# V rows by VectorE's 32x32 block transposes instead of TensorE transposes, in an attention block on one Trainium2 core

## The chip, the cores and the metric

The kernel runs on one core of one Trainium2 chip, as one program. The metric is the device time of one execution in microseconds, the median of several runs. All engines of the core work at once, each on its own queue in program order: TensorE (PE; its weight loads are shown apart as PEld), VectorE (DVE), ScalarE (ACT), GpSimd (POOL) and SyncE (SP), which here only issues DMAs. They wait for each other through semaphores.

## The reference

One transformer block with adaptive layer norm over 2048 tokens of width 512, 32 heads of 16, and a hidden layer of 1792, all in fp32:

```python
mod = (silu(c) @ w_mod)                       # six rows of 512: sa, ca, ga, sb, cb, gb
h = layernorm(x) * (1 + ca) + sa
qkv = (h @ wqkv)                              # 2048 x (3 * 32 heads * 16)
p = softmax(q @ k.T * 16 ** -0.5)             # per head, 2048 x 2048
x = x + ga * ((p @ v) @ wo)
h = layernorm(x) * (1 + cb) + sb
x = x + gb * (gelu(h @ w1 + b1) @ w2 + b2)
```

## The kernel before

Tokens are cut into NB = 4 blocks of TB = 512, heads into NG = 8 groups of four. A *unit* is one block of queries against one group of heads; there are NU = 32, in the order of query blocks, and in each 16 *steps*, one per chunk of 128 keys. Values are handled for two head groups at a time, so there are four value column sets k = 0 to 3 (128 columns, eight heads each); unit u uses set `u % 8 // 2`.

**Precision.** Projections and the later matrix products split each fp32 operand into a high and a low part and add three products (`terms3`): 12 matmuls for a 128x512 projection. In the attention phase each of them is cut into two halves of 64 rows, 24 matmuls of 64 rows.

**The script.** The first phase (about the first 100 us) is written out by hand in `SCRIPT`: tokens are names of operations (`ops`) with an engine letter. It normalizes and transposes x, projects what the first units need, and stores Q, K and V pieces to DRAM, from where they are loaded in the layout that the attention needs. Of the V projections it makes set 0: `G200`, `G201` and `G203` with `U`, `C` and `O` (transpose on TensorE, ScalarE's copy, store), and `G202` with `Y202` (`high_later`), which leaves the row block to be turned in the next phase.

**The attention phase.** `half_step(hs)` writes one step's instructions for every engine, 512 times. It holds four score matmuls `e` (L647) with ScalarE's exponentials `p` (L654), four matmuls `mx` (L390) of a later unit, whose row maxima VectorE reduces (`mxp`, L395), up to RUN = 6 background matmuls `bg` (L276) and, at its end, `pv_step`: the four heads' products with V (L681). Score, maximum and background matmuls use 64 rows each and run in pairs in the two halves of the array; the pv matmuls use all 128 rows and 32 columns each, the four heads side by side in the array's columns. Every one of them is two passes. Banks are taken in turn (`ring`, `take`): e has three, mx three, pv and bg one each.

The *background work* (`jobs`, from `work`) comes in groups of 24 half matmuls, four steps each. `block0` plans it: the rest of K and V of set 1, then Q, K and V of sets 2 and 3, then the rest of Q; weights are loaded and split two plan entries ahead. After that come the output projection and the hidden layer of earlier query blocks.

Work that follows a matmul group is put off by a clock that ticks once per exponential (four times a step): `later(n, f)` runs f n ticks on, `soon` does the same and counts it as owed, and `sides` holds work that is emitted at the end of a step, ahead of its pv matmuls.

**V, before.** `proj_v` has the projection of value set k for token block b in the order (128 columns) x (512 tokens); ScalarE copies it to `vr`; five ticks later `turn_v` waits in `sides`. It takes an mx bank, transposes four 128x128 pieces on TensorE (L335), ScalarE copies them in two instructions (L340) to `vst`, whose rows hold, for a head group and a 128-token chunk, four times 16 values and a one, and 15 zeros (VG = 83 floats). Four ticks later SP stores them to `v_d` (L345). `load_v` brings a unit's V back in two halves of 8 chunks (L601) into `vg`, two buffers in turn; each half needs the stores of its two token blocks. In `pv_step` the stationary operand of head j is the 32 columns from `j * VW`: 16 values, the one, whose product is the softmax denominator, and 15 columns that are not used.

Loads are emitted by `step_start` from the list `due`, each with the earliest step and the stores that it needs. SP issues its DMAs in program order and stands where one has to wait.

Of the kernel before, what the change touches and what calls it, by code (L numbers as in the profile page):

```python
# [8 lines left out]
F32 = mybir.dt.float32  # L9
# [22 lines left out]
VW = DH + 1  # L32
VG = 4 * VW + DH - 1
EPS = 1e-5
# [36 lines left out]
def block_kernel(ctx: ExitStack, tc: tile.TileContext, x, wqkv, wo, w1, b1, w2, b2, c, w_mod, out):  # L71
# [82 lines left out]
    wslots = [wpool.tile([P, 2, KC, P], FR, name=f"wqkv{i}") for i in range(4)]  # L154
    vst = wpool.tile([P, 2, 4, VG], F32, name="vst")
    scm, spool = pool("stage", side="right")
# [68 lines left out]
    gp.tensor_copy(sel_b, sel[:, :2, None].to_broadcast([P, 2, P]))  # L225
    gp.memset(vst[:, :, :, 4 * VW :], 0.0)
    for j in range(4):
        gp.memset(vst[:, :, :, j * VW + DH], 1.0)

# [45 lines left out]
    def mm(ps, term, i, n, r=slice(None)):  # L275
        return te.matmul(ps, term[0][r], term[1][r], start=i == 0, stop=i == n - 1)  # L276

# [22 lines left out]

    def proj_terms(w, k, b):
        hi, lo = hT[b]
        t = wt_of[w, k]
        n = range(KC)
        return terms3([t[:, 0, i] for i in n], [t[:, 1, i] for i in n], [hi[:, i] for i in n], [lo[:, i] for i in n])

# [9 lines left out]

    vrows, sides = [], []

    def proj_v(k, b):
# [10 lines left out]
    def turn_v(bk, apart=False):  # L330

        k, b, r, _ = vrows.pop(0)
        ps = take(bk)
        for t in range(4):
            te.transpose(ps[:, t * P : (t + 1) * P], r[:, t * P : (t + 1) * P], ident)  # L335

        def evac():
            p5 = ps.rearrange("p (t g j d) -> p g t j d", t=4, g=2, d=DH)
            for g in range(2):
                ac.activation(vst[:, g, :, : 4 * VW].rearrange("p t (j e) -> p t j e", e=VW)[:, :, :, :DH], p5[:, g], AF.Copy)  # L340
            return store

        def store():
            stored.add((2, k, b))
            (ac if apart else sy).dma_start(v_d[2 * k : 2 * k + 2, :, 4 * b : 4 * b + 4, :].rearrange("g p k e -> p g k e"), vst)  # L345

        if apart:
            return evac
        evac()
        soon(4, store)  # L350


# [49 lines left out]

    rows = {}

    def max_rows(u):
        m = mn[u % 2]
        ve.tensor_reduce(m[:, :16], mxp.pop(u), axis=AX.X, op=ALU.min)
        mt = small.tile([P, 32], F32, tag="mt", name="mt")
        ve.transpose(mt, m)
        m2 = small.tile([P, 2, 32], FR, tag="m2", name="m2")  # L410
        gp.tensor_copy(m2[:, 0], mt)
        gp.tensor_tensor(m2[:, 1], mt, m2[:, 0].bitcast(F32), op=ALU.subtract)

        def store():
            for i in range(2):
                sy.dma_start(m_d[u][i].rearrange("x b j -> b x j"), m2[:, i].bitcast(F32))

        def load():
            mrows.add(u)
            for a in range(2):  # L420
                r0 = a * 64 + KR
                sy.dma_start(qst[u][r0 : r0 + 2].bitcast(F32).rearrange("s p t -> s (p t)"),
                             m_d[u][:, a * 8 : a * 8 + 8].rearrange("s x b j -> s (x b j)"))
# [62 lines left out]
    def group(w, k, b):  # L486
        terms = proj_terms(w, k, b)
        keep["G", w, k, b] = ps = take("pr")
        for i, t in enumerate(terms):
            mm(ps, t, i, len(terms))  # L490

    def high(w, k, b, e):
        ps = keep["G", w, k, b]
        if w == 2:
            r = stage("vr")
            copy(e, r, ps)
            vrows.append((k, b, r, 0))
        else:
            keep["A", w, k, b] = parts = pieces("parts")
            copy(e, parts[:, 0], ps)  # L500
# [15 lines left out]
    def turn_values(w, k, b):  # L516
        keep["U"] = turn_v("pr", True)

# [39 lines left out]
    def high_later(w, k, b, e):  # L558
        r = spool.tile([P, D], F32, tag="vr", name="vr", bufs=STAGE["vr"])
        copy(e, r, keep["G", w, k, b])  # L560
        vrows.append((k, b, r, 0))
        sides.append(lambda: turn_v("mx"))

# [19 lines left out]
    assert not queue and len(vrows) == 1 and set(k[0] if isinstance(k, tuple) else k for k in keep) <= {"G", "c"}, keep  # L583
    load_w(2, 1)
# [6 lines left out]
    dvcm, dvpool = pool("div", side="right")  # L591
    vgcm, vgpool = pool("vg", bufs=2)
    ppcm, ppool = pool("p", bufs=10)
    vg, pt = {}, {}

    def load_v(u, h):
        assert all((2, u % NG // 2, b) in stored for b in (2 * h, 2 * h + 1))
        if h == 0:
            vg[u] = vgpool.tile([P, NKC, VG], F32, tag="vg", name="vg")
        sl = slice(8 * h, 8 * h + 8)  # L600
        sy.dma_start(vg[u][:, sl], v_d[u % NG][:, sl])  # L601

# [71 lines left out]
    def pv_step():  # L674
        s = cur["pv"]
        cur["pv"] += 1
        u, kc = divmod(s, NKC)
        if kc == 0:
            cur["ps"] = take("pv")
        for j in range(4):  # L680
            te.matmul(cur["ps"][32 * j : 32 * (j + 1)], vg[u][:, kc, j * VW : j * VW + 32], pt.pop(4 * s + j),  # L681
                      start=kc == 0, stop=kc == NKC - 1)
        if kc == NKC - 1:
            vg.pop(u)
            attn_out(u, cur["ps"])
# [77 lines left out]
    def until(cond):  # L763
        while not cond():
            yield None
# [203 lines left out]
    def block0():  # L969
# [13 lines left out]
        for n, (w, k, bs) in enumerate(plan):  # L983
# [6 lines left out]
            wt_of.pop((w, k))  # L990
        yield from until(lambda: not preps and not owed[0] and not vrows and not busy[0])
        open_ffn()
# [53 lines left out]
    def half_step(hs):  # L1046
# [102 lines left out]
    def step_start(s):  # L1149
# [10 lines left out]
        if kc == 0 and u + 1 < NU:  # L1160
            for h in range(2):
                need = [(2, (u + 1) % NG // 2, b) for b in (2 * h, 2 * h + 1)]
                due.append((16 * u + 2 + h, need, lambda h=h: load_v(u + 1, h)))
# [141 lines left out]
```

## Time and profile before

| | |
|---|---|
| median of 3 runs | 1686.44 us (1686.33 to 1686.57) |
| profiled execution's own time | 1688.23 us |
| its span on the core | 1686.4 us, 32218 instructions |
| mean granted TensorE clock | 0.996 |
| busy: PE, DVE, ACT, POOL | 1666.6, 1402.0, 1242.7, 691.2 us |
| mean busy share of the DMA engines (queue q1) | 50.9% |
| attention phase, first to last pv matmul | 104.9 to 1562.1 us |

The profile lists groups of instructions by line, engine, operation and tile: count, busy time in us, mean ns of one, then the idle time of the engine just before them and what ended it. Idle time of an engine that is not the bound costs nothing. A timeline row has start, duration, engine, line, operation, tiles, shape and count of merged instructions. "128*32" ahead of a shape is the array's rows times columns. A row of a source view has the least, median and greatest duration in ns behind the count.

### The profile page before, as it was taken

How to read it: one execution, taken by the hardware profiler on the slowest of the kernel's cores; microseconds unless marked ns; L12 is line 12 of the kernel's file. 1: busy time of each engine (PE TensorE's matmuls, PEld its weight loads, DVE VectorE, ACT ScalarE, POOL GpSimd, SP SyncE). 2: the span in 40 equal slices, each digit the busy share in tenths (PEclk: the TensorE clock that was granted, in tenths of full speed). 3: DMA queues.
4: the chain of work that ended last, by engine and by line, in shares of the span. 5: the costliest groups of instructions: out<-in, count | busy, mean ns of one | idle time of the engine just before them, and what ended most of it. 6: DMA issues, size and time to landing. Idle time of an engine off the chain costs nothing.

```text
span 1686.4 us, 32218 instructions
## 1 busy us (share of the span) xinstructions
PE 1666.6 (99%) x12103; PEld 915.8 (54%) x12103; DVE 1402.0 (83%) x2686; ACT 1242.7 (74%) x2386; POOL 691.2 (41%) x697
## 2 busy tenths in 40 slices
PE   7999999999999999999999999999999999999999
PEld 6655555555554455555545555555555555553777
DVE  7998888889889989888999888888999888890332
ACT  4367888878777788778877888778877788779131
POOL 7333534425121456415633456306633466226110
PEclk8999999999999999999999999999999999999999
DMA  8766766756457443425453464344363453243544
GB/s 291 220 195 186 236 194 200 227 182 206 146 159 215 121 106 102 106 67 150 123 162 88 114 165 121 84 133 134 105 181 86 116 144 101 75 119 97 209 153 157
DMA packets 137127, 251.88 MB, mean 149 GB/s; under 512 B 25854, under 2 KB 45324, under 8 KB 136972
## 3 DMA queue, kind: packets, MB, share of 16 engines
q1 hardware_dynamic: 135984, 248.53, 50.9%
q8 instruction: 96, 1.57, 0.4%
q10 hardware_dynamic: 988, 1.29, 0.3%
q14 instruction: 59, 0.48, 0.1%
HBM read 188.49 MB, written 61.28 MB: 148 GB/s over the span
## 4 chain that ended last, share of the span: by engine, by line
PE 95%; DMA 2%; DVE 1%; ACT 1%; issue 0%; POOL 0%; SPq 0%; DVEq 0%; POOLq 0%; ACTq 0%
PE bg L276 40%; PE pv L681 30%; PE e L647 16%; PE mx L390 5%; PE pr L276 2%; ACT p L654 1%; DVE mxp L395 1%; DMA wraw<-in_A_wqkv_dram 1%; PE o L276 1%; PE mx L335 0%; DMA wo<-wos 0%; DMA kh<-qk 0%; PE mx L879 0%; DMA xin<-in_A_x_dram 0%; POOL wqkv L208 0%
## 5 line engine op out<-in xcount | busy, mean ns | idle before, releaser
L395 DVE TENSOR_REDUCE mxp<-mx 128x1 f32<-128x512 f32 x2034 | 1286.4, 683 | 145.7 <-PE mx L390 131.4
L654 ACT ACTIVATE p<-e 128x512 f32<-128x512 f32 x2048 | 1072.8, 608 | 272.2 <-PE mx L390 251.4
L390 PE MATMUL mx<-kh,qst 48*128 48x512 f32 x2034 | 836.6, 423 | 0.7 <-DVE mxp L395 0.5
L647 PE MATMUL e<-qst,kh 50*128 50x512 f32 x2048 | 779.2, 424 | 3.2 <-ACT p L654 3.2
L647 PEld LDWEIGHTS e<-qst,kh 50*128 50x128 f32 x2048 | 341.8, 185 | 431.5 <-ACT p L654 310.2
L681 PE MATMUL pv<-p,vg 128*32 128x512 f32 x4096 | 547.2, 605 | 0.3 <-ACT osb L668 0.3
L390 PEld LDWEIGHTS mx<-kh,qst 48*128 48x128 f32 x2034 | 368.2, 185 | 14.2 <-DVE mxp L395 8.3
L276 PE MATMUL bg<-w,g 64*128 64x512 f32 (+1 forms) x1056 | 264.3, 389 | 0.8 <-issue 0.8
L276 PEld LDWEIGHTS bg<-w,g 64*128 64x128 f32 (+1 forms) x1056 | 196.0, 186 | 30.0 <-issue 1.2
L276 PE MATMUL bg<-pchi,w 64*128 64x512 f32 (+1 forms) x656 | 177.6, 391 | 0.0
L681 PEld LDWEIGHTS pv<-p,vg 128*32 128x32 f32 x4096 | 81.1, 108 | 173.0 <-issue 160.3
L276 PE MATMUL bg<-hThi,wqkv 64*128 64x512 f32 x560 | 153.1, 392 | 0.0
L276 PEld LDWEIGHTS bg<-pchi,w 64*128 64x128 f32 (+1 forms) x656 | 120.9, 185 | 23.9 <-DVE tick L1091 4.2
L276 PEld LDWEIGHTS bg<-hThi,wqkv 64*128 64x128 f32 x560 | 103.7, 185 | 12.7
L923 POOL TENSOR_SCALAR s<-s 128x512 f32<-128x512 f32 x40 | 59.9, 1497 | 90.3 <-ACT s L921 89.6
L942 POOL TENSOR_TENSOR x<-y,x 128x512 f32<-128x512 f32 x28 | 36.0, 1286 | 144.6 <-ACT y L941 128.7
L276 PE MATMUL bg<-pclo,w 64*128 64x512 f32 (+1 forms) x328 | 88.9, 389 | 0.0
L276 PE MATMUL bg<-hTlo,wqkv 64*128 64x512 f32 x280 | 76.5, 392 | 0.0
L276 PEld LDWEIGHTS bg<-pclo,w 64*128 64x128 f32 (+1 forms) x328 | 60.0, 184 | 13.5 <-DVE tick L1091 4.2
L916 POOL TENSOR_TENSOR s<-h 128x512 f32<-128x512 f32 x40 | 41.7, 1042 | 61.7 <-ACT h L915 61.7
L276 PE MATMUL bg<-wo,pchi 64*128 64x512 f32 x192 | 59.5, 389 | 0.4 <-DMA wo<-wos 0.4
L276 PEld LDWEIGHTS bg<-hTlo,wqkv 64*128 64x128 f32 x280 | 51.6, 184 | 7.5
(163 smaller groups left out, 1322.9 us busy)
## 6 DMA issues: line engine op xcount, KB each, us to landing
kh<-qk SPq DMA_DIRECT2D x256, 192.0 KB
w<-w1s SPq DMA_DIRECT2D x56, 512.0 KB
w<-w2s SPq DMA_DIRECT2D x54, 512.0 KB
vg<-v SPq DMA_DIRECT2D x64, 332.0 KB
qk<-parts SPq DMA_DIRECT2D x32, 512.0 KB
qst<-qk SPq DMA_DIRECT2D x64, 192.0 KB
qk<-parts SPq DMA_DIRECT2D x32, 256.0 KB
ou<-osb SPq DMA_DIRECT2D x32, 256.0 KB
```

The source lines that it names most:

```text
L276: return te.matmul(ps, term[0][r], term[1][r], start=i == 0, stop=i == n - 1)
L390: te.matmul(ps, qst[u][r0 : r0 + KR, p, qc * P : (qc + 1) * P], kh(u, kr // 2)[r0 : r0 + KR, p, (kr % 2) * TB : (kr % 2 + 1) * TB], start= ...
L395: ins = ve.tensor_reduce(mxp[u][:, hc, kr : kr + 1], ps, axis=AX.X, op=ALU.max, negate=True)
L647: ins = te.matmul(ps, kh(u, kc // 8)[r0 : r0 + KX, p, (kc % 8) * P : (kc % 8 + 1) * P], qst[u][r0 : r0 + KX, p], start=True, stop=True)
L654: op = ac.activation(t, ps, AF.Exp, scale=SCALE)
L681: te.matmul(cur["ps"][32 * j : 32 * (j + 1)], vg[u][:, kc, j * VW : j * VW + 32], pt.pop(4 * s + j), start=kc == 0, stop=kc == NKC - 1)
L916: gp.tensor_tensor(s, h, h, op=ALU.mult)
L923: gp.tensor_scalar(s, s, 1.0, None, op0=ALU.add)
L942: later(4, lambda: gp.tensor_tensor(x2[t], y, x2[t], op=ALU.add))
```

## The change

For thirteen of the sixteen V groups (the twelve of the attention phase and the one that the script leaves over) the transposes move from TensorE to VectorE, which turns 32x32 blocks inside SBUF. So that four blocks side by side end in rows that belong to one token chunk, the projection reads its tokens in another order: 16 runs of 32 tokens per matmul (`proj_terms(..., blocks=True)`, `mm`). `turn_block` turns one quarter of a group (128x128) with one VectorE instruction; `turn_blocks` is called at the end of each step, ahead of the pv matmuls, and spreads a group's four quarters over up to three steps, later when a unit's row maxima have just been emitted (`rowed`). The store follows two ticks after the last quarter.

The rows' layout changes too: four chunks are interleaved, so the 32 stationary columns of a head lie four floats apart in `vst`, `v_d` and `vg`, and a chunk's two heads take 2 * 17 floats with no padding. `vst` has two buffers after the script. `v_d` is one tensor per value set; sets 1 to 3 are stored with the block index leading and loaded in two DMAs by head pairs, each of which needs all four token blocks; set 0 is loaded in two halves of two token blocks. The two `vg` tiles are allocated once, with 60 zero floats at their ends. The three script groups that stay on TensorE write the new layout with ScalarE.

```diff
-v_d = dram.tile([NG, P, NKC, VG], F32, name="v")
+v_d = [dram.tile([4, P, NB, 4 * VB], F32, name=f"v{k}") for k in range(KC)]     # VB = 2 * VW
...
+    def store_v(k, b, apart=False):
+        stored.add((2, k, b))
+        t = vst[b % len(vst)]
+        rows = v_d[k][:, :, b]
+        if k:
+            sy.dma_start(rows.rearrange("q p e -> p q e"), t)
+        elif apart:
+            ac.dma_start(rows.rearrange("i p e -> p i e"), t)
+        else:
+            for i in range(4):
+                sy.dma_start(rows[i].rearrange("(q a) e -> a q e", q=4), t[32 * i : 32 * (i + 1)])
...
     def proj_v(k, b):
         def evac(ps):
             r = stage("vr")
             ac.activation(r, ps, AF.Copy)
-            vrows.append((k, b, r, clock["t"]))
-            later(5, lambda: sides.append(lambda: turn_v("mx")))
-        return proj_terms(2, k, b), "bg", evac
+            later(2, lambda: blocked.extend((k, b, r, q) for q in range(4)))
+            until_hs[0] = None
+        return proj_terms(2, k, b, True), "bg", evac
+
+    def turn_block():
+        k, b, r, q = blocked.pop(0)
+        ve.transpose(vst[b % len(vst)][:, q].rearrange("p (j d k) -> p k j d", j=2, d=VW)[:, :, :, :DH],
+                     r[:, q * P : (q + 1) * P].rearrange("p (k j d) -> p k j d", k=4, j=2))
+        if q == 3:
+            soon(2, lambda: store_v(k, b))
+
+    def turn_blocks(hs):
+        if not blocked:
+            return
+        if until_hs[0] is None:
+            until_hs[0] = hs + 2
+        left = until_hs[0] - hs
+        n = len(blocked)
+        rowed_now = rowed[0] >= clock["t"] - 4
+        for _ in range(n if left <= 0 else 0 if rowed_now and n <= 2 * left else -(-n // (left + 1))):
+            turn_block()
...
     def load_v(u, h):
-        sl = slice(8 * h, 8 * h + 8)
-        sy.dma_start(vg[u][:, sl], v_d[u % NG][:, sl])
+        k, i = u % NG // 2, u % 2 * 2
+        rows = vg[u % 2][:, :VX].rearrange("p (i b e) -> p i b e", i=2, b=NB)
+        if k:
+            i += h
+            sy.dma_start(rows[:, h], v_d[k][:, 32 * i : 32 * (i + 1)].rearrange("q a b e -> q a (b e)"))
+        else:
+            bs = slice(2 * h, 2 * h + 2)
+            sy.dma_start(rows[:, :, bs], v_d[k][i : i + 2, :, bs].rearrange("i p b e -> p i (b e)"))
...
     def pv_step():
         for j in range(4):
-            te.matmul(cur["ps"][32 * j : 32 * (j + 1)], vg[u][:, kc, j * VW : j * VW + 32], pt.pop(4 * s + j),
+            n = ((j // 2 * NB + kc // 4) * 2 + j % 2) * 4 * VW + kc % 4
+            te.matmul(cur["ps"][32 * j : 32 * (j + 1)], vg[u % 2][:, n : n + 125 : 4], pt.pop(4 * s + j),
                       start=kc == 0, stop=kc == NKC - 1)
...
         if sides and not (had and act["g"] is None):
             sides.pop(0)()
+        turn_blocks(hs)
```

More of the change, by code (lines that the diff above doesn't have):

```diff
@@ L225, in block_kernel @@
     gp.tensor_copy(sel_b, sel[:, :2, None].to_broadcast([P, 2, P]))
[L226 to L228 removed]
+    gp.memset(vst[0].rearrange("p q (j d k) -> p q j d k", j=2, d=VW)[:, :, :, DH], 1.0)
     def mod_part(ps, i):
@@ L337, in evac @@
         def evac():
[L338 to L350, printed above, removed]
+            for j in range(2):
+                ac.activation(vst[b % len(vst)].rearrange("p i (j d k) -> p k i j d", j=2, d=VW)[:, :, :, j, :DH],
+                              ps.rearrange("p (k i j d) -> p k i j d", k=4, i=4, j=2)[:, :, :, j], AF.Copy)
+            return lambda: store_v(k, b, True)
+        return evac
     qst, mxp = {}, {}
@@ L582, in block_kernel @@
             ops[name](*[int(i) for i in ids], *([{"a": ac, "v": ve, "g": gp}[e]] if e else []))
-    assert not queue and len(vrows) == 1 and set(k[0] if isinstance(k, tuple) else k for k in keep) <= {"G", "c"}, keep
+    assert not queue and not vrows and len(blocked) == 4 and set(k[0] if isinstance(k, tuple) else k for k in keep) <= {"G", "c"}, keep
     load_w(2, 1)
@@ L990, in block0 @@
             wt_of.pop((w, k))
-        yield from until(lambda: not preps and not owed[0] and not vrows and not busy[0])
+        yield from until(lambda: not preps and not owed[0] and not blocked and not busy[0])
         open_ffn()
@@ L1161, in step_start @@
             for h in range(2):
-                need = [(2, (u + 1) % NG // 2, b) for b in (2 * h, 2 * h + 1)]
+                need = [(2, (u + 1) % NG // 2, b) for b in range(NB)]
                 due.append((16 * u + 2 + h, need, lambda h=h: load_v(u + 1, h)))
```

49 lines of the change are left out of this document (28 added, 21 removed).

## Prediction, made before the changed kernel was run

> **What bounds the kernel now.** I read the page first (engine shares, then the chain that ended last), then TensorE's timeline step by step, then the rows of the operations that the change touches.
>
> ```profile
> PE 1666.6 (99%) x12103; PEld 915.8 (54%) x12103; DVE 1402.0 (83%) x2686; ACT 1242.7 (74%) x2386; POOL 691.2 (41%) x697
> ...
> PE 95%; DMA 2%; DVE 1%; ACT 1%; issue 0%; POOL 0%; SPq 0%; DVEq 0%; POOLq 0%; ACTq 0%
> ...
> L681 PE MATMUL pv<-p,vg 128*32 128x512 f32 x4096 | 547.2, 605 | 0.3 <-ACT osb L668 0.3
> ```
>
> TensorE is busy 99% of the span and makes up 95% of the chain, so a microsecond added to or taken from its instruction stream is, to first order, a microsecond of the kernel. The pv line matters because the change rewrites its weight loads: 4096 instructions are 512 steps of 8 (four heads, each matmul in two passes). Now the pace of the steps, around one of the turns that go (PE timeline):
>
> ```profile
> 122.08 1.06 PE L681 MATMUL pv<-p,vg 128*32 128x512 f32 x8
> ...
> 124.60 0.40 PE L390 MATMUL mx<-kh,qst 48*128 48x512 f32 x1
> 124.99 0.66 PE L335 MATMUL mx<-ident,vr 128*128 128x128 f32 x4
> 125.58 1.06 PE L681 MATMUL pv<-p,vg 128*32 128x512 f32 x8
> 128.43 1.06 PE L681 MATMUL pv<-p,vg 128*32 128x512 f32 x8
> ...
> L335 PE MATMUL mx<-ident,vr x52: 272/273/329, 102.3 to 372.3; 128*128 128x128 f32 x52
> ```
>
> A step without a turn lasts 128.43 - 125.58 = 2.85 us; the step with one lasts 125.58 - 122.08 = 3.50 us. Four transposes cost 0.65 us of the path, of which nothing is hidden.
>
> **The change, part by part.**
>
> *Turns removed.* The 52 transposes of that row are 13 groups of four: the twelve V groups of the attention phase and the one that the script leaves over. The twelve turns in the script before it stay on TensorE. 13 x 0.65 = 8.4 us less. Each group's two ScalarE copies into vst go too, 26 x 0.38 us; ScalarE at 74% is not the bound and the steps with these copies (125.58 to 128.43) are no longer than others, so I take 0 for them.
>
> *V rows strided.* This term decides. The 32 weight columns of a pv matmul now lie 16 bytes apart instead of side by side. The rows of the weight loads:
>
> ```profile
> L681 PEld LDWEIGHTS pv<-p,vg x4096: 105/108/151, 104.9 to 1561.6; 128*32 128x32 f32 x196
> L276 PEld LDWEIGHTS bg<-w,g x1056: 183/185/189, 686.1 to 1682.2; 64*128 64x128 f32 x136, 128*128 128x128 f32 x40
> L681 PE MATMUL pv<-p,vg x4096: 592/616/1061, 104.9 to 1562.1; 128*32 128x512 f32 x196
> 702.11 0.16 PEld L681 LDWEIGHTS pv<-p,vg 128*32 128x32 f32 x8 [0.36 <-issue]
> ```
>
> 96 columns more take 185 - 108 = 77 ns: 0.80 ns a column, 26 ns for the 32. The weight loads of a step cannot run ahead: they start at 702.11 after 0.36 us of standing. And their 26 ns are seen on the path: a pv matmul lasts 592 at the least and 616 in the median, 24 ns more, which I read as the first pass waiting for its columns (the second pass loads under the first). So whatever the stride adds to one load is paid once in each of the 512 steps. No trace row shows a strided weight load. The nearest rows are other engines reading one element per 64 bytes from SBUF (the query and key weights, read with their head and dimension axes swapped) against plain rows:
>
> ```profile
> L192 ACT ACTIVATE wqkv<-wraw x13: 621/1099/1109, 37.2 to 413.1; 128x512 fp32r<-128x512 f32 x13
> L194 POOL CAST wqkv<-wraw x3: 1032/1066/1067, 17.7 to 33.2; 128x512 fp32r<-128x512 f32 x3
> L615 POOL CAST wsp<-wf 128x512 fp32r<-128x512 f32 x32 | 19.6, 612 | 40.9 <-DMA wf<-in_B_w_dram 39.7
> L208 DVE TENSOR_TENSOR wqkv<-wraw,wqkv x1: 1027/1027/1027, 35.9 to 35.9; 128x512 fp32r<-128x512 f32 x1
> L911 DVE TENSOR_TENSOR g<-h,g x16: 691/693/1151, 1568.4 to 1662.5; 128x512 fp32r<-128x512 f32 x16
> ```
>
> ScalarE's longer ones are the swapped reads, its shortest the plain V weights: (1099 - 621) / 512 = 0.93 ns more an element; GpSimd (1066 - 612) / 512 = 0.89; VectorE (1027 - 693) / 512 = 0.65. Three engines of different plain pace all end near 1.7 to 2.1 ns an element, which looks like the memory and not the engine. For 32 columns that is 21 to 30 ns, times 512 steps 10.7 to 15.2 us. I take 27 ns, 13.8 us. The lower end is 0 (if weight loads do not pay it); below nothing is excluded, since strided reads were slower on all three. The upper end: the four heads' columns are loaded at once (8 loads within the 0.16 us above); if strided they must go one after the other, 128 columns at 0.83 instead of 32 add 80 ns a step, 41 us.
>
> A page of the Trainium skill, Advanced Engine Details and Errata, section SBUF Cachelines, speaks against the change: lines are 16 bytes, and at least two hits on a line are needed to absorb the access latency, so a step of 16 bytes pays on every element; the rows above agree for a step of 64 bytes, and no run here yet shows it for a weight load.
>
> *V projections in runs of 32.* 288 half-height matmuls of the attention phase and 12 full ones of the script read their moving rows in 16 runs of 128 bytes. No matmul here reads in runs. The nearest row is ScalarE writing vst in 16 runs of 16:
>
> ```profile
> L340 ACT ACTIVATE vst<-mx 128x256 f32<-128x256 f32 x26 | 8.6, 384 | 0.4 <-PE mx L335 0.2
> L668 ACT ACTIVATE osb<-pv 128x512 f32<-128x512 f32 x32 | 19.2, 601 | 12.5 <-PE pv L681 12.3
> ```
>
> 256 elements in runs take 217 ns less than 512 in one piece, 0.85 ns an element, the pace of the whole 512 if some 166 ns are fixed: runs cost nothing there. One lost element per run would be 16 x 0.85 = 14 ns, 300 of them 4 us, less where two halves of the array run together. I take 0; ends 0 and 4.
>
> *VectorE's 52 transposes of 128x128.* The rows next to it:
>
> ```profile
> L409 DVE STREAM_TRANSPOSE mt<-mn x32: 211/211/214, 91.8 to 1518.5; 128x32 f32<-128x32 f32 x32
> L395 DVE TENSOR_REDUCE mxp<-mx x2034: 627/681/694, 47.4 to 1517.4; 128x1 f32<-128x512 f32 x185
> ...
> 129.01 0.68 DVE L395 TENSOR_REDUCE mxp<-mx 128x1 f32<-128x512 f32 x1
> 129.99 1.89 DVE L395 TENSOR_REDUCE mxp<-mx 128x1 f32<-128x512 f32 x3 [0.30 <-PE mx L390]
> ```
>
> From 32 to 512 elements the two operations differ by (681 - 211) / 480 = 0.98 ns an element, so 128 elements take 211 + 96 x 0.98 = about 305 ns, if the strided writing is free; if each written element costs the 0.65 to 0.93 ns that strided reads cost above, up to 424 ns. The cover is the 0.30 us in which VectorE waits for TensorE in every step. Three reductions in 1.89 us (0.60 apart, 0.68 long) show that successive instructions overlap by 0.08, so a transpose takes 0.23 to 0.34 us of it. One per step hides. At the one or two steps per group where two are emitted, 0.45 to 0.7 us delay the next step's first reduction by 0.15 to 0.4. Behind it waits TensorE's fourth mx of that step, which needs the bank of the first (three banks): the first reduction ends 130.67, 2.24 us after the pv of 128.43; the fourth mx starts 2.52 after its pv (124.60 against 122.08). That leaves 0.28. So the price is 0 to 12 x 0.12 = 1.5 us; I take 0.
>
> *The last values come later.* A V group's store used to follow its turn by four exponentials; now the blocks may be spread over two more steps, and for head groups 2 to 7 both loads of a unit need all four token blocks, where the first half needed two. Only the last V group is near its use, in unit 6, whose first pv set is that of 386.87:
>
> ```profile
> 378.17 1.06 PE L681 MATMUL pv<-p,vg 128*32 128x512 f32 x8
> ...
> 386.87 1.07 PE L681 MATMUL pv<-p,vg 128*32 128x512 f32 x8
> ...
> 370.99 1.18 SPq L416 DMA_DIRECT2D m<-m  x2
> 373.63 0.58 SPq L422 DMA_DIRECT2D qst<-m  x2
> ...
> 376.60 0.43 SPq L345 DMA_DIRECT2D v<-vst  x1
> ...
> 384.29 0.34 SPq L601 DMA_DIRECT2D vg<-v  x1
> ```
>
> The script's arithmetic (two half steps allowed after the first) puts the last blocks into the step that ends with the pv of 378.17. VectorE reaches them after that step's last reduction, 1.3 us after such a pv starts (129.69 against 128.43), and is through 0.3 to 0.8 later; the store is issued some 2.0 us after 378.17. From a store's issue to the load that waits for it this trace has 373.63 - 370.99 = 2.6 us for 16 KB twice, and 384.29 - 376.60 = 7.7 for V itself. Two load issues and a landing follow, 2.5 to 3 us if a load lands as the small store did. That is 7 to 13 us after 378.17, and TensorE wants it 8.7 us after: a stall of 0 to 4 us, once. I take 1.0. SP stands in that wait with the loads of kh, qst and the weight pieces queued behind it, as it stood in the V load's wait before (that of 384.29); nothing there was late for TensorE.
>
> *The rest, taken at 0.* V's stores and loads carry 136 instead of 166 floats per partition and token piece (less traffic, off the path); the store of the script's leftover group is four issues instead of one (three more at about 0.4 us each on SP, as in the issues above, long before the second half of unit 0 needs them); a few memsets on GpSimd, busy 41%; the script's three remaining ScalarE turns write with the 16 byte step, 6 x 256 x 0.93 ns = 1.4 us at most if they lay on the path.
>
> **The sum.** -8.4 (turns) + 13.8 (strided weights) + 1.0 (unit 6) = +6.4 us. The profiled execution took 1688.23 us, a span of 1686.4 and 1.8 around it, so it would become 1694.6; it stood 1.8 above the median of the runs, 1686.44, which becomes 1692.8. Bounds of this case: the low ends give -8.4 + 10.7 = +2.3, the high ends -8.4 + 15.2 + 4 + 1.5 + 4 + 1.4 = +17.7, so 1688.7 to 1704, most of it under 1699.
>
> **The rivals.**
>
> *Weight loads do not pay the stride: faster.* For it: a weight column takes 0.80 ns whatever the instruction, so the load may be paced by the array and the memory may keep up; the three rows that pay are of 64 bytes, not 16, and none is TensorE's. Against it: those rows end at 1.7 ns and more an element, twice the 0.80. Then -8.4 + 1.0 = -7.4: 1679.0, with 1677.5 to 1685 by the other terms. It decides below 14 ns per load (7.4 / 512). In the Trainium skill, TensorE: Matmul & The Clock Gate, section LDWEIGHTS, the time is the number of columns over 1.2 GHz, with no word of their distance; by that rule alone this rival holds, and the trace agrees with its 27 ns for 32 columns side by side.
>
> *The four heads' strided loads share one read path: much slower.* For it: eight loads now start within 0.16 us, so four read together, each from another address of the same partitions. Against it: the four matmuls behind them also read four addresses at once at full pace. Price 41 us for 80 ns: -7.4 + 41 = +33.6, 1720.
>
> *A partial penalty cancels the gain: no change.* 8 to 20 ns per load, 4 to 10 us against 7.4: within 0.2% of before, at 1686.
>
> *VectorE becomes the bound in the V groups,* if a block takes over 0.45 us: then the first two cases end up to 1.5 us higher, which the ranges hold.
>
> **How the numbers follow.** Strided weights at about the price of the other engines: 0.39. No price: 0.33. Shared path: 0.17. Cancelled: 0.11. A measurement can tell about 0.2%, 3.4 us, from no change. Faster 0.34 (the second case, a little of the last); within it 0.13; slower 0.53. The likeliest gives 1692.8; the range 1677.5 to 1699 holds the first, second and last case, 0.8 in all, and leaves out the shared path.
>
> **What would show it.** Steps with a turn vanish: twelve of 3.50 us become 2.85 to 2.9, 52 transposes gone from mx. The weight loads of pv: 108 ns stays (rival), or grows by some 27 (forecast) or 80, and the plain step from 2.85 us to 2.88 or 2.93 everywhere, also long after the last V group; that is the sign of this term, as the turns' is confined to the first 375 us. DVE transposes of 128x128 at 305 to 424 ns, with TensorE's waits on mxp no larger. PE's wait for a DMA of vg before unit 6's first pv, 0 to 4 us. The prediction fails if the pv weight loads do not change, or if the plain step grows by more than 0.05 us.

## Result and profile after

The changed kernel takes 1727.79 us in the median of 5 runs (1724.13 to 1729.35), the kernel before 1686.44 (1685.03 to 1687.88). The ratio is 1.0242, 95% interval 1.0227 to 1.0257: slower by 41 us. The forecast of 1692.8 had the direction and missed the size; 1727.79 lies above the range. The profiled execution took 1729.35 us with a span of 1727.3, against 1688.23 and 1686.4, so the profile has 40.9 us to account for.

From the page of the changed kernel: busy times, the granted clock in 40 slices, the chain that ended last, and two groups (busy time, mean ns, then the idle time ahead of them and what ended it).

```profile
PE 1686.8 (98%) x12051; PEld 941.8 (55%) x12051; DVE 1415.1 (82%) x2738; ACT 1236.7 (72%) x2360; POOL 690.9 (40%) x696
...
PEclk9999999998999999999999999999999999999999
...
PE 90%; DMA 4%; DVE 3%; ACT 2%; issue 0%; SPq 0%; POOL 0%; ACTq 0%
...
L716 PE MATMUL pv<-p,vg 128*32 128x512 f32 x4096 | 569.4, 624 | 13.2 <-DMA vg<-v 12.9
...
L716 PEld LDWEIGHTS pv<-p,vg 128*32 128x32 f32 x4096 | 112.8, 148 | 191.2 <-issue 179.7
```

PE's part of the chain fell from 95% to 90%; DMA doubled to 4%. The pv matmuls now wait 12.9 us for the load of vg, which they never did. PE is busy 20 us longer with 52 fewer instructions: its instructions got longer, so some of the loss is pace (or clock) and not waiting.

The places show in TensorE's timeline. These are all the rows with an idle time over 1 us between 100 and 1600 us, and the 0.71 behind the longest (brackets: idle before, what ended it); before had none.

```profile
115.36 1.93 PE L716 MATMUL pv<-p,vg 128*32 128x512 f32 x4 [3.08 <-DMA vg<-v]
...
190.32 0.79 PE L681 MATMUL e<-qst,kh 50*128 50x512 f32 x1 [3.54 <-ACT p L688]
...
299.27 0.79 PE L681 MATMUL e<-qst,kh 50*128 50x512 f32 x1 [2.25 <-ACT p L688]
...
409.89 1.93 PE L716 MATMUL pv<-p,vg 128*32 128x512 f32 x4 [9.13 <-DMA vg<-v]
412.54 1.93 PE L716 MATMUL pv<-p,vg 128*32 128x512 f32 x4 [0.71 <-DMA vg<-v]
...
561.35 0.79 PE L278 MATMUL bg<-wo,pchi 64*128 64x512 f32 x1 [1.54 <-DMA wo<-wos]
```

The durations matter as much as the brackets: 1.93 for a pv row that takes 1.1 elsewhere, 0.79 for an e that takes 0.40. A table by stretch shows why (start:end, length, busy time and count of PE, PEld, DVE, ACT and POOL, granted clock, DMA share, GB/s):

```profile
108.00:114.00 6.00, 4.28 (x30) 1.85 (x27) 4.44 (x10) 4.43 (x9) 3.48 (x4) 1.00 0.28 56
114.00:121.00 7.00, 5.64 (x22) 2.59 (x26) 2.43 (x5) 2.28 (x4) 3.04 (x3) 0.51 0.78 211
...
189.00:196.00 7.00, 5.68 (x23) 2.85 (x25) 2.59 (x6) 4.91 (x9) 6.62 (x10) 0.52 0.44 157
...
404.00:418.00 14.00, 7.39 (x26) 2.82 (x30) 2.25 (x5) 2.28 (x4) 3.77 (x4) 0.51 0.62 194
...
600.00:1600.00 1000.00, 997.18 (x7544) 531.61 (x7544) 859.25 (x1674) 800.86 (x1549) 452.90 (x443) 1.00 0.44 115
```

Around each of the waits the granted clock is 0.5: for 6.8 us at the first three, for 13.7 us at unit 6 (5.6 of them while TensorE still stands) and for 3.4 us at the last. So a wait of 3 us costs 6.5. Between 600 and 1600 us there is neither such a wait nor a slow clock.

Comparing the start of each of the 512 pv sets with the same set before gives the whole account:

| | us |
|---|---|
| pace of every step: +9.49 from step 150 to 510, +10.55 without one unrelated step (164, where *before* has a stretch of half clock and the changed kernel hasn't), so 0.029 a step, times 512 | +15.0 |
| twelve steps without their turn, 0.66 each | -7.9 |
| wait and slow clock, steps 2 to 3 | +6.5 |
| the same, steps 25 to 26 | +6.5 |
| the same, steps 61 to 62 | +5.4 |
| the same, unit 6, steps 95 to 96 | +14.2 |
| the same, steps 146 to 147 | +2.9 |
| start +0.5, the unrelated step -1.1, tail -0.9 | -1.5 |
| sum (span: +40.9) | +41.1 |

So there are two questions: what sets the pace (15), and what makes the five waits (35.5).

### The profile page after: what moved, and what is told of

It is laid out like the page before. It is cut to its first block, busy times and chain, and to the rows that moved or that the text cites. A ratio compares the mean times of both kernels' runs of the same rounds, so it can differ in the third digit from the quotient of the medians.

```text
span 1727.3 us, 32193 instructions
## 1 busy us (share of the span) xinstructions
PE 1686.8 (98%) x12051; PEld 941.8 (55%) x12051; DVE 1415.1 (82%) x2738; ACT 1236.7 (72%) x2360; POOL 690.9 (40%) x696
## 4 chain that ended last, share of the span: by engine, by line
PE 90%; DMA 4%; DVE 3%; ACT 2%; issue 0%; SPq 0%; POOL 0%; ACTq 0%
PE bg L278 37%; PE pv L716 29%; PE e L681 17%; PE mx L415 4%; ACT p L688 1%; DVE mxp L420 1%; DMA wraw<-in_A_wqkv_dram 1%; PE pr L278 1%; DVE hTlo L510 1%; DMA vg<-v 1%; PE o L278 1%; DMA kh<-qk 1%; DMA v<-vst 1%; DMA wm<-in_w_mod_dram 1%; DMA wo<-wos 0%; DVE bst L236 0%
## 5 line engine op out<-in xcount | busy, mean ns | idle before, releaser
L716 PE MATMUL pv<-p,vg 128*32 128x512 f32 x4096 | 569.4, 624 | 13.2 <-DMA vg<-v 12.9
L716 PEld LDWEIGHTS pv<-p,vg 128*32 128x32 f32 x4096 | 112.8, 148 | 191.2 <-issue 179.7
L278 PE MATMUL bg<-hThi,wqkv 64*128 64x512 f32 x560 | 157.0, 400 | 0.0
```

The source lines that it names most:

```text
L278: return te.matmul(ps, term[0][r], rhs, start=i == 0, stop=i == n - 1)
L716: te.matmul(cur["ps"][32 * j : 32 * (j + 1)], vg[u % 2][:, n : n + 125 : 4], pt.pop(4 * s + j), start=kc == 0, stop=kc == NKC - 1)
```

## The experiments

### The pace: is it the distance of the weight columns?

Three kernels are *before* with one edit (shortened here), the distance of the 32 weight columns of pv; loads, stores and turns stay. The window is shifted so that it stays inside the loaded half, so the columns read are not those of V.

```diff
-vg[u][:, kc, j * VW : j * VW + 32]
+vg[u].rearrange("p c e -> p (c e)")[:, n : n + 31 * s + 1 : s]     # s = 2, 4, 16 floats
```

> The kernel before, with the 32 weight columns of every pv matmul read 16 bytes apart instead of side by side (the wrong columns, so the attention's values are not the reference's; the denominators still are sums of the weights); nothing else changes. In the changed kernel the pv weight load takes 146 ns instead of 108 and the plain step 2.874 us instead of 2.843. Theory: the step of 16 bytes alone makes that, 512 x 0.031 = +15.9 us, 1702.3 us, with weight loads near 146 ns and no stalls. Rival of the prediction (four heads share one read path, 80 ns): +41 us, 1727, which would be the whole loss. If the longer loads come from elsewhere (VectorE writing rows, DMA traffic): 1686.4 and 108 ns.

> As the run with 16 bytes, with the columns 8 bytes apart. If a 16 byte line serves two columns and that is enough: 108 ns, 1686.4 us within 0.15%. If any step costs, or the cost is per line read: between 108 and 146 ns and 1688 to 1702.

> As the run with 16 bytes, with the columns 64 bytes apart. If one column per line is the whole cost: again 146 ns and 1702 us. If the distance counts beyond the line (as ScalarE's 0.93 ns an element at 64 bytes may be, 30 ns more per load): more than 146 ns, up to 160, and up to 1710.

Measured against before: columns 8 bytes apart 1687.59 us, ratio 1.0002 (0.9993 to 1.0012); 16 bytes 1703.03, 1.009 (1.0073 to 1.0106); 64 bytes 1701.49, 1.0082 (1.0067 to 1.0097). The weight loads of the three, in that order (least, median and greatest ns):

```profile
L683 PEld LDWEIGHTS pv<-p,vg x4096: 106/110/119, 105.7 to 1562.7; 128*32 128x32 f32 x196
```

```profile
L683 PEld LDWEIGHTS pv<-p,vg x4096: 134/144/169, 104.3 to 1579.9; 128*32 128x32 f32 x196
```

```profile
L683 PEld LDWEIGHTS pv<-p,vg x4096: 131/150/180, 105.1 to 1574.1; 128*32 128x32 f32 x196
```

and in the changed kernel:

```profile
L716 PEld LDWEIGHTS pv<-p,vg x4096: 134/146/174, 105.4 to 1603.4; 128*32 128x32 f32 x196
```

The 16-byte distance alone, with nothing else of the change, costs 15.2 us by the ratio, the same 15 as in the account, and the load lasts 36 ns longer (38 in the changed kernel). 8 bytes cost nothing; 64 cost no more than 16. So, of the distances tried, the cost comes between 8 and 16 bytes and doesn't grow beyond. This is the pace, shown.

### The waits: loads whose leading dimension is four

The changed kernel's loads for sets 1 to 3 lead with four blocks of 32 partitions (`q a b e`, q = 4), set 0's with 128 partitions. In the trace the 256 packets of the two loads issued at 402.85 run from 404.19 to 411.95, 7.76 us; the sum of their own times is 4.0 times that, so four are under way at a time. Before, the 128 packets of one half last 1.54 us (385.26 to 386.80) with 12.7 under way. The Trainium skill, DMA: Bandwidth & Descriptors, section on why a DMA increments its semaphore by 16, says that the number of engines is taken from the slowest dimension of the two access patterns; the trace agrees, with 4.0 for a dimension of four. The stores of sets 1 to 3 aren't spread over four: their 512 packets mostly run about 14 at a time and last 1.0 to 1.2 us (1.9 at 251.2), nearly as before; the last one, at 397.5, comes in two parts.

What such a load does to its neighbours is seen at 190 us. SP's queue in the changed kernel (start and duration of an issue), then ScalarE:

```profile
176.69 1.20 SPq L631 DMA_DIRECT2D vg<-v  x2
...
178.45 0.58 SPq L189 DMA_DIRECT2D wraw<-in_A_wqkv_dram  x1
```

```profile
188.72 1.07 ACT L193 ACTIVATE wqkv<-wraw 128x512 fp32r<-128x512 f32 x1 [3.87 <-DMA wraw<-in_A_wqkv_dram]
189.69 1.55 ACT L688 ACTIVATE p<-e 128x512 f32<-128x512 f32 x3
```

The two V loads are under way until 186.76. The weight load issued behind them lands only by 188.72; ScalarE, in program order, stands 3.87 us for it ahead of three exponentials, and TensorE stands 3.54 us for those. V's own values are not late there at all: V's loads make *another* load late. At 299 us it is the same again: two V loads under way from 288.28 to 295.76, wraw issued behind them at 288.65, ScalarE standing 2.56 us for it until 297.66.

Two kernels change the changed kernel. The first stores and loads all sets as set 0 (loads by 128 partitions, four store issues), the second puts the columns side by side and leaves the loads. The edits are shortened.

```diff
-        if k: sy.dma_start(rows.rearrange("q p e -> p q e"), t)       # a1: store_v as for set 0,
-        elif apart: ...                                               # load_v as for set 0
+        if apart: ...
```

> The changed kernel with sets 1 to 3 stored and loaded as its set 0 is: four store DMAs per group, two loads per unit by halves of the token blocks, with 128 partitions as the slowest dimension; the rows stay strided and both loads still need all four token blocks. Theory: the loads take 2 to 4 us instead of 5 to 12, the stalls at steps 26, 62 and 148 go (6.6 + 5.3 + 3.5 us, with the halved clock after them), the one at 96 to 98 (11.4 us) shrinks to 3 to 8 because the store still comes late, the one at step 3 (3.8 us) stays: about 1727.8 - 15.4 - 6 = 1706, between 1702 and 1711. Rival (the stalls come from the late blocks on VectorE or from the order of DMAs, not from the loads' width): 1724 or more.

Measured 1710.79, ratio to before 1.0131 (1.0116 to 1.0146). The waits of steps 25 to 26, 61 to 62 and 146 are gone (+0.7, 0 and +0.3 us are left), those of step 2 (+4.3) and unit 6 (+10.0) are not. TensorE's rows of this kernel:

```profile
184.80 0.49 PE L675 MATMUL e<-qst,kh 50*128 50x512 f32 x1 [0.26 <-ACT p L682]
...
391.23 1.93 PE L710 MATMUL pv<-p,vg 128*32 128x512 f32 x4 [3.90 <-DMA vg<-v]
```

```diff
-vst[...].rearrange("p (j d k) -> p k j d", ...)                       # a2: four chunks interleaved
+vst[...].rearrange("p (k j d) -> p k j d", ...)
-vg[u % 2][:, n : n + 125 : 4]
+vg[u % 2][:, n : n + 32]
```

> The changed kernel with rows in which a head's columns lie side by side (blocks written to runs of 16 values instead of every fourth float); loads unchanged. Theory: pv weight loads back at 108 ns and plain steps at 2.843 us, 15.9 us less; the stall at step 3 goes too (3.8 us), because an odd head's 32 columns then run into the next token block's rows only at the last chunk of a block: 1727.8 - 19.7 = 1708, with the four stalls of the loads left, 1704 to 1712. VectorE's transposes nearer 305 ns than 398. Rival (stride not the cause of the longer steps): 1724 to 1728.

Measured 1712.12, 1.0139 (1.0123 to 1.0155). This is just above the 1704 to 1712 expected. The weight loads are back at 108 ns and the step at its old pace. All waits stay, that of step 2 too (+6.4), where I had expected it to go; only that of step 146 is smaller (1.16 us for 1.54, costing 0.8 for 2.9). The one at 190 us in this kernel:

```profile
189.00 0.79 PE L681 MATMUL e<-qst,kh 50*128 50x512 f32 x1 [3.50 <-ACT p L688]
```

So the two causes are separate: 15.7 us are the distance, 17.0 us the way of storing and loading, by the medians. By the ratios to *before*, which took 1.7 us longer in the runs beside these two, it is 17.4 and 18.7.

The opposite test puts four blocks into *before*. A first try had no effect on the packets: the four blocks lie end to end in DRAM, and its loads are still 128 packets in about 1.5 us. Its time says nothing on the question.

> The kernel before with each load of V (from its DRAM copy to vg) written with four blocks of 32 partitions as its slowest dimension, as the changed kernel's loads of sets 1 to 3 are; same bytes, same places, output unchanged. In the changed kernel these loads' packets run about four at a time and last 5 to 12 us, and TensorE stands behind them at 26, 62, 98 and 148 steps. Theory: the shape of the load confines it to few DMA engines, loads of 332 KB last 5 to 13 us, the query and key weights queued behind them come late, and stalls (with a halved clock after them) cost 5 to 25 us: 1692 to 1711. Rival: loads that long are still hidden and only the late store makes the stalls: 1686.4 within 0.2%.

Measured 1686.98, 0.9998 (0.9989 to 1.0007). A second try leaves a gap between the blocks, and stores in four pieces:

```diff
-v_d = dram.tile([NG, P, NKC, VG], F32, name="v")
+v_d = dram.tile([NG, 4, 33, NKC, VG], F32, name="v")
-        sy.dma_start(vg[u][:, sl], v_d[u % NG][:, sl])
+        sy.dma_start(vg[u][:, sl], v_d[u % NG][:, :32, sl])
```

> The kernel before, with V's DRAM copy in four blocks of 32 partitions with a gap after each (the gap keeps the four blocks from merging into one run of 128 rows, as they did in four_before), stored in four pieces and loaded in one DMA per half whose slowest dimension is these four blocks. Theory: a load's packets run four at a time, 332 KB last 8 to 12 us instead of 1.5 to 5, what is queued behind them (wraw, kh, qst, wo) comes late and TensorE stands at some of these places: 5 to 20 us, 1692 to 1707. Rival: the long loads are hidden in this kernel, as halves are loaded apart: 1687 within 0.2%.

Measured 1711.66, 1.0146 (1.0131 to 1.0162): 25 us, more than I had expected. The loads now mostly last 5 to 7 us each with under four packets at a time, and TensorE stands where before it never did. Its longest wait, then VectorE and SP's queue:

```profile
427.52 0.79 PE L391 MATMUL mx<-kh,qst 48*128 48x512 f32 x1 [11.69 <-DVE mxp L396]
```

```profile
426.57 0.35 DVE L730 RECIPROCAL dn<-dn 128x32 f32<-128x32 f32 x1 [12.36 <-DMA dn<-ou]
```

```profile
411.34 1.03 SPq L602 DMA_DIRECT2D vg<-v  x1
...
413.63 0.54 SPq L602 DMA_DIRECT2D vg<-v  x1
414.26 1.14 SPq L721 DMA_DIRECT2D dn<-ou  x1
```

TensorE stands 11.69 us at a matmul that has nothing to do with V. It waits for VectorE, and VectorE waits for softmax denominators (dn), whose load was issued behind two V loads; the packets of those run from 413.8 to 419.2 and from 420.0 to 425.8. So loads with a leading four make waits by themselves, without the transposes and the stride. The four store issues are in this kernel too; how much of the 25 us is theirs wasn't separated. But the kernel with all sets loaded by 128 partitions has the four issues as well, its stores mostly last longer (1.5 to 2.3 us), and yet it loses the waits at 190 and 299 us: those waits follow the loads and not the stores.

### What is left: the two waits for V itself

Both edits together:

> Both edits together: only the moved turn, the runs of 32, the later blocks and the loads' need of all four blocks are left of the change. Theory: 1727.8 - 15.9 - 3.8 - 15.4 - 6 = 1686.7, that is -8.4 for the turns against before and 5 to 9 for the late unit 6, 1683 to 1692. If TensorE loses something else to VectorE's transposes or the runs of 32: above 1692.

Measured 1697.25, 1.005 (1.0035 to 1.0065), not the 1686.7 expected. Left are steps 2 to 3 (+6.9), unit 6 (+9.0) and step 146 (+2.9). The halves of this kernel's loads are cut by token block, but each is still held back until all four blocks are stored. The next kernel lets each half wait for its own two blocks only:

```diff
-need = [(2, (u + 1) % NG // 2, b) for b in range(NB)]
+need = [(2, (u + 1) % NG // 2, b) for b in (2 * h, 2 * h + 1)]
```

> Both edits, and each half of a unit's V is loaded as soon as its own two token blocks are stored, as before the change. Theory: the first half of unit 6 is there long before, the second is needed 8 steps later, so that stall goes as well: the turns' 8.4 us less than before and nothing against it, 1678.5, between 1677 and 1682. Rival: V blocks on VectorE delay TensorE in the V groups: 1682 to 1688, with V steps longer than 2.85 us.

Measured 1694.43, 1.0038 (1.0023 to 1.0052): missed again, with 1678.5 expected. The rival doesn't explain it either: the loss is in two waits, +6.8 and +8.3, and not in longer steps of the V groups. TensorE, and SP's issue of the second half for the same unit:

```profile
112.80 1.92 PE L710 MATMUL pv<-p,vg 128*32 128x512 f32 x4 [3.02 <-DMA vg<-v]
...
389.96 1.92 PE L710 MATMUL pv<-p,vg 128*32 128x512 f32 x4 [4.93 <-DMA vg<-v]
```

```profile
386.93 0.38 SPq L629 DMA_DIRECT2D vg<-v  x1
```

Each time only four of the eight pv matmuls (x4) wait, and they wait for a load that was issued as the unit's first steps already ran: the *second* half, whose values they don't read. In `vg` the order is head pair, token block. A half by token blocks is two pieces, and from the start of the first to the end of the second lies the other head pair's first half. The theory was that the wait is put in for that whole stretch. The test gives each half a stretch of its own (560 floats):

```diff
-rows = vg[u % 2][:, :VX].rearrange("p (i b e) -> p i b e", i=2, b=NB)
+rows = vg[u % 2][:, 560 * h : 560 * h + VX // 2]
```

> As a4_halves, with the two halves of a unit's V (token blocks 0-1 and 2-3) in two separate stretches of the vg tile, 560 floats each, so that a load of the second half and the pv matmuls of the first touch no common range. In a4_halves the two losses left are at steps 2 and 96, each where the load of a second half is emitted while the unit's first steps run: +6.8 and +8.3 us, the halved clock included. Theory: the pv matmuls after the emission wait for that load because its two pieces per partition span the other head pair's first half; with separate stretches both waits go: 1694.4 - 6.8 - 8.3 = 1679.3, between 1677 and 1682, 0.4 to 0.5% under before. Rival (the second half is truly late for its first step): the wait moves to steps 7 to 8 and 103 to 104 and most of the 15 us stays, 1688 to 1694.

Measured 1683.11 (11 runs), 0.9979 (0.997 to 0.9988): faster than before by 0.21%, 1.1 us above the range expected. Both waits are gone, as the theory has it, and neither moved to later steps. But one is new, at steps 101 to 102 (+5.6). VectorE, TensorE and SP of this kernel:

```profile
397.86 0.35 DVE L757 RECIPROCAL dn<-dn 128x32 f32<-128x32 f32 x1 [3.23 <-DMA dn<-ou]
```

```profile
398.81 0.79 PE L413 MATMUL mx<-kh,qst 48*128 48x512 f32 x1 [2.56 <-DVE mxp L418]
```

```profile
375.88 2.29 SPq L330 DMA_DIRECT2D v<-vst  x4
382.58 0.38 SPq L629 DMA_DIRECT2D vg<-v  x1
...
392.82 0.59 SPq L748 DMA_DIRECT2D dn<-ou  x1
```

VectorE stands for a load of softmax denominators that SP issued at 392.82, behind V's store and the load that waits for its landing. Two ways to give it room: have VectorE come to the reciprocal later, or have SP not stand.

```diff
-        later(11 if over[0] else 14, inv)     # a6: four ticks later
+        later(11 if over[0] else 18, inv)
```

> As a5_apart, with VectorE's reciprocal of the denominators (o_prep) emitted 18 ticks after its load instead of 14, one step later. In a5_apart one loss against before is left, 5.6 us at steps 101 and 102: VectorE stood 3.23 us for the load of dn, which shared the queues with unit 6's second V load (391 to 397 us), so the mx banks were not freed, TensorE stood 2.56 us and then ran at half clock. Theory: with the reciprocal a step later the load has landed and the loss goes: 1683.1 - 5.6 = 1677.5, between 1676 and 1680, and only the turns' 12 to 13 x 0.65 us are left as the difference to before. Rival: the same wait appears at another late transfer (kh or qst), 1681 to 1685.

Measured 1685.3 (11 runs), 0.9988 (0.9979 to 0.9997): missed. The rival named another transfer, and it didn't hold as written either: it is the same load. It went out later too (397.60), and VectorE stood again:

```profile
401.48 0.35 DVE L757 RECIPROCAL dn<-dn 128x32 f32<-128x32 f32 x1 [3.07 <-DMA dn<-ou]
```

This wait costs 4.4 us (steps 103 to 104), less than the 5.6. That the kernel is slower all the same shows at its end: 12 more matmuls stand behind the last pv set (533 for 521), and from the start of that set to the end takes 128.5 us for 124.8. So a later reciprocal also pushed background work to the end.

```diff
-            soon(2, lambda: store_v(k, b))                # a7: store later, and its loads later
+            soon(8, lambda: store_v(k, b))
-        stored.add((2, k, b))
+        later(8 if k else 0, lambda: stored.add((2, k, b)))
```

> a5_apart with V's store emitted 8 ticks after a set's last block instead of 2, and, for sets 1 to 3, the loads that need it let go 8 ticks later still, so that SP reaches the store after VectorE has written the rows and reaches the loads after the store has landed. In a5_apart SP stood 5.6 us for VectorE's vst and 4.4 us for the landing at 375.88 to 382.58, and the load of dn behind them was issued about 8 us late. Theory (SP's standing in V's own store and loads makes dn late): the wait for dn at steps 101 to 102 goes with its 5.6 us, 1677.5 us, within 1676 to 1680. Rival (SP is late for other reasons and some load or other will be late): the wait moves or stays, 1681 to 1686; if V's own load comes too late for unit 6 instead, the wait shows at steps 95 to 96.

Measured 1678.37, 0.9945 (0.9932 to 0.9959): faster than before by 0.55%, within the expectation. SP's waits for VectorE's rows, in total, times and longest, in the kernel with separate stretches and in this one:

```profile
SPq L330 <- DVE vst L345: 51.4, 12, 9.6
```

```profile
SPq L330 <- DVE vst L345: 11.7, 4, 6.1
```

and this kernel's page and SP queue:

```profile
PE 1657.8 (99%) x12051; PEld 912.7 (54%) x12051; DVE 1411.9 (84%) x2738; ACT 1234.0 (74%) x2360; POOL 690.6 (41%) x696
```

```profile
386.53 0.88 SPq L748 DMA_DIRECT2D dn<-ou  x1
```

The load of denominators goes out 6.3 us earlier (386.53 for 392.82), VectorE no longer makes TensorE stand there, and TensorE has no idle time over 1 us left between 100 and 1600 us. The step account of this kernel against before is nearly all turns: twelve of -0.64 to -0.74, which with the start (+0.7) make -7.3 by step 91; behind that +0.7 at step 146 and -1.1 at the unrelated step, and a tail 1.0 shorter. One of VectorE's transposes now takes 300 ns in the median instead of 398; its rows have no 16-byte step any more.

## Why the prediction was right or wrong

The prediction named two signs of being wrong, unchanged weight loads and a step that grows by more than 0.05 us. Neither came; what failed lay outside of them, in the transfers.

*Turns, -8.4: right,* -7.9 measured. Twelve steps lost 0.59 to 0.72 us each, 0.66 in the mean once the slower pace is taken out. The thirteenth, the one left over from the script, doesn't show: the start is 0.5 us later, not 0.65 earlier. It can't be told, as the start differs by -0.6 to +0.9 us in the three column kernels, whose script is that of before. The timeline of pv in the changed kernel, where the step from 129.38 is that which had the turn:

```profile
129.38 1.10 PE L716 MATMUL pv<-p,vg 128*32 128x512 f32 x8
132.25 1.10 PE L716 MATMUL pv<-p,vg 128*32 128x512 f32 x8
135.14 1.09 PE L716 MATMUL pv<-p,vg 128*32 128x512 f32 x8
```

It is 2.87 us long, as its neighbour is (2.89).

*Strided weights, +13.8: right,* 15.0 in the account and 15.2 alone, but in part by luck. I took 27 ns a load and said that all of it is paid in each step; the load grew by 38 and the step by 29, so some of it is hidden, and the two errors nearly cancel. The estimate came from other engines' reads 64 bytes apart, and 64 and 16 bytes do cost nearly the same here. One argument behind it fell: I read a pv median of 616 ns over the least of 592 as the first pass waiting for its columns. With columns 8 bytes apart the median is 593, at the same step:

```profile
L683 PE MATMUL pv<-p,vg x4096: 592/593/624, 105.7 to 1563.1; 128*32 128x512 f32 x196
```

With 64 bytes it is 593 too, at the longer step, so that difference says nothing.

Two rules of the Trainium skill stood against each other. That of Advanced Engine Details and Errata, SBUF Cachelines (16-byte lines, two hits needed) agrees with 110 ns at 8 bytes, 144 at 16 and 150 at 64. That of TensorE: Matmul & The Clock Gate, LDWEIGHTS (columns over 1.2 GHz) doesn't: the same 32 columns took 108 to 150 ns, and its 27 ns agreed only with the difference between 128 and 32 columns, not with a whole load. The rival built on it, no price, is refuted. So is the shared path: the step grew by 29 ns, not 80, and that the time came near its 1720 has another cause.

*Runs of 32, 0: right.* The groups bg<-hThi,wqkv have a mean of 400 ns for 392 before, which holds the stretches at half clock; between 130 and 180 us, at full clock and with V groups among them, a matmul lasts 393 for 392.

*VectorE's transposes hidden, 0: right.* 398 ns in the median, inside 305 to 424:

```profile
L347 DVE STREAM_TRANSPOSE vst<-vr x52: 378/398/407, 106.7 to 393.1; 128x128 f32<-128x128 f32 x52
```

and the steps that carry them are no longer than others. TensorE's idle time that VectorE's reductions end is 0.5 us in all, as before.

*The script's three turns with the 16-byte step, 0 with 1.4 at most:* six ScalarE copies take 658 ns in the median for 384, so 1.6 us in all, a little over that end. Within what the start differs by, they don't show on the path.

*Unit 6, +1.0: this step failed,* with 14.2. The chain that I wrote down was there, link by link, and came to 7 to 13 us, a stall of 0 to 4, of which I took 1.0. Its first and last links were priced too short. SP's queue in the changed kernel:

```profile
395.68 0.43 SPq L327 DMA_DIRECT2D v<-vst  x1
402.85 1.11 SPq L631 DMA_DIRECT2D vg<-v  x2
```

The pv of the reference step is at 391.90. The store is issued 3.8 us after it (said: 2.0). The loads follow 7.2 later (said: 2.6 to 7.7, so this link holds, at its long end, V's own row). The pv matmuls go on 7.0 and 9.7 us after that, for the 2.5 to 3 that I took for a landing from a store of 16 KB twice; here it is 272 KB twice, with four packets at a time. 18.0 us against 8.9 that were free gives the wait of 9.13. And no term of mine had the halved clock: 8.1 us of it lie behind the wait, about 4 us lost at half speed by this estimate.

*"Less traffic, off the path" and "nothing there was late for TensorE": this step failed too,* and with the wait of step 2 they make the other 21.3 us. I counted bytes (136 floats for 166) and not the shape of the transfer. What stood behind V's loads then came late: wraw at steps 25 and 61 (11.9 us), and wo at 146 (2.9). The wait of step 2 (6.5) is a different one. I had put the four store issues of the script's leftover group at 0, "long before the second half of unit 0 needs them". But readers of the *first* half waited for it, as the load of the second half covers, from its first to its last byte, values that it doesn't bring. And I named what is queued behind SP's wait for the landing, but not that SP would stand for VectorE's rows: 54.5 us in the changed kernel (L327) against 17.2 for ScalarE's before:

```profile
SPq L327 <- DVE vst L347: 54.5, 11, 8.4
```

```profile
SPq L345 <- ACT vst L340: 17.2, 5, 4.9
```

What this costs in the changed kernel itself was not tried; in the kernel with separate stretches it was 4.7 us (1683.11 to 1678.37).

With its two failed terms put right the sum is -7.9 + 15.0 + 14.2 + 21.3 - 1.5 = 41.1. The idea itself, transposes off TensorE, is worth 8.1 us (1686.45 to 1678.37) once columns, transfers and queue are as before; the layout that came with it cost six times that.

One thing stays open, the wait for wo at step 146 (2.9 us). It is in every kernel here: 0.40 us before, 0.86 with columns 8 bytes apart, 0.62 with all sets loaded by 128 partitions, 0.87 in the last kernel, 1.54 in the changed one. Only in the changed kernel and in the one with both edits did 3.4 us of half clock come with it, and only there does it cost 2.9. What makes wo later is not settled, so these 2.9 us are put down to the transfers by argument only.

## What to carry to other kernels

When an operation is moved to an engine with room, price the layout that it brings, not the operation: how far apart the bound engine's columns lie, over which dimension each transfer is spread, what range it covers, and who stands in a queue for it. A wait of 2 to 4 us on TensorE cost about twice its length here when the clock was halved with it (3.08 us cost 6.5, 2.25 cost 5.4), and it is often not at the moved data but at whatever is queued behind it. And a chain of waits is priced by the row of the same operation and size, or by its long end.

## What was not expected of the hardware

- The distance of weight columns costs as a step: side by side 108 ns, 8 bytes 110, 16 bytes 144, 64 bytes 150, for 32 columns of 128 rows.
- How long TensorE stands doesn't alone say whether the clock is halved. 2.25 us at 299 brought 6.8 us of 0.5. In the kernel with all sets loaded by 128 partitions, 3.2 us at 115.6 brought none, as its stretch behind the wait shows:

```profile
115.60:122.00 6.40, 6.33 (x48) 3.31 (x48) 4.43 (x10) 3.98 (x8) 1.69 (x2) 1.00 0.73 190
```

- The clock also halved without such a wait: before, behind three of 0.2 to 0.8 us from 571 to 577, for 3.4 us at 578.0 (0.57 over 578 to 582); and in the kernel with columns 16 bytes apart, at the same place, for 13.7 us. This is the step that differs by 1.1 us in the account. The same three waits stand in all fourteen profiles, and the clock halved behind them in these two only.
